# A scan and two MLPs on one core: the due times of the planner's steps moved, and its transfers planned longer

## The chip, the cores and the metric

The kernel runs on one core of a Trainium2 chip. Its engines are TensorE (PE in the profile, with its weight loads as PEld), VectorE (DVE), ScalarE (ACT), GpSimd (POOL) and SyncE (SP), which here issues the transfers. The metric is the device time of one execution in microseconds; three runs of the kernel before have a median of 625.69 us (624.65 to 625.95).

## The reference

```python
def reference(**kwargs):
    attn_out = _attn_ref(x, a, B, C)                     # (4, 8, 768, 32)
    x = attn_out.transpose(0, 2, 1, 3).reshape(3072, 256)
    x = _moe_ref(x, w_in, w_out)       # h = x @ w_in; g = h if h > 0 else exp(h) - 1; g @ w_out   (d_ff 2048)
    return _moe2_ref(x, w_a, w_b, w_out2)                # (x @ w_a * (x @ w_b)) @ w_out2           (d_ff 1536)
```

`_attn_ref` is a linear recurrence over the sequence for 4 batches and 8 heads: state = decay * state + B x, and y = C state, with 16 states and 32 values a head, worked out chunk by chunk: inside a chunk y is (C B^T * L) x with L the decays between two positions under the causal mask, and from the chunk before comes C state times a decay. All is fp32; the second and third part are matrix products over 3072 tokens.

## The kernel before

**The work.** The scan is cut into 24 units u (a chunk of 128 positions, 6 of them, by 4 batches). A unit builds the decays in a tile ab (DVE, L575, two halves), takes their last column (le, ACT, L590) for POOL's product xe (L595), multiplies C and B on PE (L616 for the first 8 units, L629 for the others, four heads at a time, both halves into one PSUM bank, cbank), lets DVE multiply that bank into ab (mask, L632), and forms y and the new state in the bank ybank (L663, L667, L671), from where x is written (L703, or L706 and L709 as a high and a low part). Four units make one tile of 512 tokens of x, and there are 6 tiles. Phase A is the first MLP: each tile has 8 pairs of 256 hidden units; PE's up products (L738, L739, L741: high times high, high times low, low times high; tile 0 in whole fp32, L729), exp on ACT (L837), minus one (L841), the choice of the two branches on DVE (L847), a high part on ACT (L851), a low part on POOL or DVE (L858, L856), and PE's down products into acc (L750, L751, L754). Phase B is the second MLP with Strassen products: 18 groups, each with products of three matmuls (L1139 to L1141) into four banks (ybank, cbank and the two acc), which ACT copies out (keep, L1151) or DVE adds out (plus, L1159); then the gate (L1168, L1171, L1174), the down products (L1079, L1080, L1083), and evictions (L1108, L1110).

**Beside it.** The weights are loaded as raw words into tiles called raw and fx, scaled by ACT (L427, into an m), prepared by ACT or DVE (L434, L430), put together by POOL or DVE (L439), and split into high and low parts (L384, L388). B and C of the units from 8 on are split into bf16 parts as well: a raw load, casts on ACT (L476), rests on POOL (L479), stores into a DRAM tensor called parts (L484, 128 KB each), and from there one load sm a unit (L523, 512 KB). Each unit from 8 on also loads ab from DRAM (L537, 512 KB). PE has filler matmuls for the start (L319).

**What sets the order.** None of this is in the order of the code. The class Plan takes every step (`add`) with a planned length on each engine that could do it, its predecessors and a due time. `emit` then plays the program through with these lengths: of the steps that are ready it picks the one with the smallest `(floor(start / 0.25), due, index)`, gives it to the engine on which it ends first, and writes its instructions at once. So the planned lengths and the due times decide the order of each engine's queue, and each engine executes its queue in that order. What waits at the head of a queue holds up all that is behind it. The table MOVE shifts due times by the part of the program and the step's name; it is empty before. The planned length of a transfer is in the branch for SP: a latency, its KB over 310 and 0.05, one after the other, eight at most outstanding.

Of the kernel before, what the change touches and what calls it, by code (L numbers as in the profile page):

```python
# [63 lines left out]
class Plan:  # L64
# [38 lines left out]
    def emit(self, go=True):  # L103
        n = len(self.steps)
        self.work = {}
        left, then, ends = [0] * n, [[] for _ in range(n)], [None] * n
        for i, s in enumerate(self.steps):
            for a in set(s[2]):
                left[i] += 1
                then[a].append(i)  # L110
        free = dict.fromkeys(("PE", "ACT", "DVE", "POOL", "SP"), 0.7)
        port, dma, done = 0.0, 0.0, 0
        landed = []
        self.log = []
        ready = []

        def enter(i):
            engines, fn, after, due, prt, pad, weight, nb = self.steps[i]
            opts = []
            for e, c in engines.items():  # L120
                at = nb
                for a in after:
                    end, ea = ends[a]
                    end += (self.SYNC[ea] if ea != e else self.SAME[e]) + (pad if ea != e else 0.0)
                    if end > at:
                        at = end
                opts.append((e, c, at))
            ready.append((due, i, opts, prt))

        for i in range(n):  # L130
            if not left[i]:
                enter(i)
        while ready:
            best = None
            for k, (due, i, opts, prt) in enumerate(ready):
                end = None
                for e1, c1, at in opts:
                    s1 = free[e1] if free[e1] > at else at
# [12 lines left out]
            due, _, _, prt = ready.pop(k)  # L151
            if e == "PE":
                if self.fill and go and start < FILL_TO and start - free["PE"] > 0.2:
                    k0 = int(free["PE"] / self.TICK)
                    rate = 1.0 if k0 > 0 and self.work.get(k0 - 1, 0.0) >= 0.5 else 0.5
                    m = int((start - free["PE"] - 0.2) * rate / 0.054)
                    self.fill(m)
                    self.pe_clock(free["PE"], 0.055 * m, 1.0)
                end = self.pe_clock(start, c, self.steps[i][6])
                free[e] = end  # L160
            elif e == "SP":
                end = start
                for kb in c:
                    if len(landed) >= 8:
                        end = max(end, landed[-8])
                    dma = max(dma, end + 1.5) + kb / 310.0 + 0.05
                    landed.append(dma)
                    end += 0.46
                free[e], end = end, dma
            else:  # L170
                end = start + c
                free[e] = end - self.LAG[e]
                if e == "POOL" or prt:
                    port = end
# [14 lines left out]
def kernel(  # L189
# [14 lines left out]
    nc = tc.nc  # L204
# [89 lines left out]
    add = plan.add  # L294
# [166 lines left out]
    def split_bc(m, s, j, due):  # L461
        cols = slice(512 * j, 512 * j + 512)
        rb = raw[1] if s == 1 else nxt(raw, "raw")
        t = rb.ap[:, 0:512].bitcast(F32)
        part = [rb.ap[:, 512 + 256 * i:768 + 256 * i].bitcast(BF16) for i in range(3)]

        slots = ([(0, 3)], [(3, 3)], [(6, 2)]) if m == 0 else ([(0, 3, 2), (6, 0, 0)],) * 3

        def load(e):
            nc.sync.dma_start(t, (bt, ct)[m][P * s:P * (s + 1), cols])  # L470

        last = i_load = add({"SP": [256]}, load, rb.take(), due=due - 8, nb=due - 12)
        rb.users.append(i_load)
        for i in range(3):
            def cast(e, i=i):
                nc.scalar.copy(part[i], t)  # L476

            def rest(e, i=i):
                eng[e].tensor_sub(t, t, part[i])  # L479

            def store(e, i=i):
                dst = parts[s].rearrange("r m (n k) f -> r m n k f", k=8)
                for k in ([[0, 1, 2], [3, 4, 5], [6, 7]][i] if m == 0 else [k for k in range(8) if k % 3 == i]):
                    nc.sync.dma_start(dst[:, m, :, k, cols], part[i])  # L484

            i_c = add({"ACT": 0.62}, cast, last, due=due)
            k = 3 if (i < 2) else 2
            i_s = add({"SP": [128] * k}, store, i_c, due=due)
            i_parts.setdefault(s, []).append(i_s)
            rb.users += [i_c, i_s]  # L490
            if i < 2:
                last = add({"POOL": 1.3}, rest, i_c, due=due, port=True)
                rb.users.append(last)
# [7 lines left out]
    def unit(u, due):  # L501
# [69 lines left out]
        for g in range(2):  # L571
# [71 lines left out]
        if c > 0:  # L643
# [99 lines left out]
    def down(ph, t, f, gh, gl, i_h, i_l, due):  # L743
# [51 lines left out]
    def pair(t, p):  # L795
# [78 lines left out]
        def downs():  # L874
            if quad:
                for f in range(4):
# [6 lines left out]
                    i_down["A", 0] = [add({"PE": 0.89}, dn_q, i3, i_m["w_out", 0], d, due=due + PAIR1 + 0.1 * f)]  # L883
# [513 lines left out]
```

## Time and profile before

| | |
|---|---|
| three runs | 625.69 us median, 624.65 to 625.95 |
| profiled execution | 627.16 us, of which the span of the instructions is 625.5 us |
| PE busy | 608.7 us, 97% of the span |
| ACT, DVE, POOL busy | 375.6, 374.4, 321.6 us |
| mean granted clock of TensorE | 0.991 |
| transfers | 59.94 MB, nearly all in the first 275 us |

The profile is of one execution, so sums over its rows are compared with its own 627.16 us, and its distance to the median (1.47 us) is taken off at the end. PE is busy nearly all of the time, so what is of interest is where it is not, and where its clock is not at 1.00: the page's slices show such places before 200 us and in the last slice. From 275 to 600 us PE has no idle time at all.

### The profile page before, as it was taken

The page shows a single profiled execution, that of the slowest core. Times are in us where ns is not written, and L with a number is a line of the kernel's source. Part 1 is how long each engine was busy: PE and PEld are TensorE (multiplying, and loading weights), DVE is VectorE, ACT ScalarE, POOL GpSimd, SP SyncE. Part 2 cuts the span into 40 slices and gives each one's busy share as a digit, 9 for nine tenths or more (in the row PEclk, how much of TensorE's full clock was granted, in tenths as well). Part 3 has the DMA queues.
Part 4 walks back from the last instruction along what each step waited for, and adds up shares of the span by engine and source line. Part 5 has one row for each costly group of instructions (what it writes and reads, how often), then busy time and mean ns, then how long its engine had stood idle before and what let it go on. Part 6 is the DMA issues. An engine that isn't in the chain of part 4 may idle for free.

```text
span 625.5 us, 9248 instructions
## 1 busy us (share of the span) xinstructions
PE 608.7 (97%) x3533; PEld 480.8 (77%) x3533; DVE 374.4 (60%) x515; ACT 375.6 (60%) x536; POOL 321.6 (51%) x245
## 2 busy tenths in 40 slices
PE   9999997999969999999999999999999999999996
PEld 8864455777857877778888888888888888888885
DVE  7875755876737786788544676556533357433333
ACT  2656575567756757657776765547554456554553
POOL 3353373457755456343452576666555555555552
PEclk9999997999989999999999999999999999999999
DMA  8947743777558655400000000000100000100001
GB/s 250 331 130 256 243 136 118 245 224 242 176 206 301 226 195 193 138 4 1 1 1 0 1 1 1 0 1 1 68 0 2 1 1 1 68 1 0 1 0 68
DMA packets 33404, 59.94 MB, mean 96 GB/s; under 512 B 2736, under 2 KB 13904, under 8 KB 33360
## 3 DMA queue, kind: packets, MB, share of 16 engines
q1 hardware_dynamic: 33360, 59.35, 28.5%
q8 instruction: 28, 0.46, 0.3%
q14 instruction: 16, 0.13, 0.1%
HBM read 47.61 MB, written 11.73 MB: 95 GB/s over the span
## 4 chain that ended last, share of the span: by engine, by line
PE 87%; DMA 5%; ACT 3%; DVE 1%; issue 1%; SPq 1%; POOL 1%; POOLq 0%; ACTq 0%; DVEq 0%
PE acc L754 6%; PE acc L750 6%; PE acc L751 6%; PE up L738 6%; PE up L739 5%; PE up L741 5%; PE up L1083 5%; PE up L1080 5%; PE up L1079 5%; PE acc L1140 4%; PE acc L1141 4%; PE acc L1139 4%; PE ybank L1140 3%; PE cbank L1140 3%; PE ybank L1141 3%; PE ybank L1139 3%
## 5 line engine op out<-in xcount | busy, mean ns | idle before, releaser
L858 POOL TENSOR_TENSOR gl<-e,gh 128x1024 fp32r<-128x1024 f32 x20 | 49.0, 2448 | 62.0 <-ACT gh L851 57.4
L1168 DVE TENSOR_TENSOR x<-x 128x512 f32<-128x512 f32 x36 | 29.0, 807 | 74.2 <-POOL x L1212 73.7
L1174 POOL TENSOR_TENSOR gl<-x,gh 128x512 fp32r<-128x512 f32 x35 | 48.9, 1400 | 35.9 <-ACT gh L1171 35.9
L750 PE MATMUL acc<-gh,hi_w_out 128*128 128x512 f32 x160 | 63.7, 398 | 0.0
L837 ACT ACTIVATE e<-up 128x1024 f32<-128x1024 f32 x44 | 45.1, 1025 | 29.9 <-PE up L741 23.6
L1212 POOL TENSOR_TENSOR x<-e,x 128x512 f32<-128x512 f32 x36 | 45.8, 1292 | 33.4 <-ACT e L1151 29.4
L751 PE MATMUL acc<-gh,lo_w_out 128*128 128x512 f32 x160 | 62.8, 393 | 0.0
L754 PE MATMUL acc<-gl,hi_w_out 128*128 128x512 f32 x160 | 51.8, 400 | 0.0
L841 ACT ACTIVATE e<-e,bias 128x1024 f32<-128x1024 f32 x44 | 50.8, 1154 | 1.0
L575 DVE TENSOR_TENSOR_SCAN ab<-ab,delta 128x512 f32<-128x512 f32 x36 | 49.0, 1372 | 0.4 <-DMA ab<-a_seg 0.4
L847 DVE SCALAR_TENSOR_TENSOR up<-e,up 128x512 f32<-128x512 f32 x40 | 27.8, 695 | 26.5 <-ACT e L841 25.7
L847 DVE SCALAR_TENSOR_TENSOR e<-e,up 128x512 f32<-128x512 f32 x48 | 30.7, 681 | 18.9 <-ACT e L841 18.9
L1174 POOL TENSOR_TENSOR gl<-p,gh 128x512 fp32r<-128x512 f32 x18 | 23.9, 1327 | 34.6 <-issue 31.6
L738 PE MATMUL up<-xh,hi_w_in 128*128 128x512 f32 x96 | 41.2, 430 | 0.0
L739 PE MATMUL up<-xh,lo_w_in 128*128 128x512 f32 x96 | 38.4, 400 | 0.0
L1159 DVE TENSOR_TENSOR p<-acc,p 128x512 f32<-128x512 f32 x36 | 24.3, 688 | 22.0 <-PE acc L1141 22.0
L1079 PE MATMUL up<-gh,hi_w_out 128*128 128x512 f32 x96 | 37.4, 389 | 0.0
L1080 PE MATMUL up<-gh,lo_w_out 128*128 128x512 f32 x96 | 37.4, 389 | 0.0
L632 DVE TENSOR_TENSOR ab<-cbank,ab 128x512 f32<-128x512 f32 x35 | 24.0, 687 | 20.2 <-PE cbank L629 11.9
L750 PEld LDWEIGHTS acc<-gh,hi_w_out 128*128 128x128 f32 x160 | 30.5, 190 | 6.7 <-issue 0.2
L751 PEld LDWEIGHTS acc<-gh,lo_w_out 128*128 128x128 f32 x160 | 30.4, 190 | 6.3
L439 POOL TENSOR_TENSOR m<-m,raw 128x1024 int32<-128x1024 int32 x11 | 27.6, 2511 | 14.1 <-DVE m L430 9.8
(295 smaller groups left out, 1690.5 us busy)
## 6 DMA issues: line engine op xcount, KB each, us to landing
ab<-a_seg SPq DMA_DIRECT2D x18, 512.0 KB
parts<-raw SPq DMA_DIRECT2D x64, 128.0 KB
sm<-parts SPq DMA_DIRECT2D x16, 512.0 KB
p<-in_xb SPq DMA_DIRECT2D x20, 256.0 KB
raw<-in_w_out SPq DMA_DIRECT2D x4, 1024.0 KB
fx<-in_w_out SPq DMA_DIRECT2D x3, 1024.0 KB
out_t<-m SPq DMA_DIRECT2D x12, 256.0 KB
raw<-in_w_in SPq DMA_DIRECT2D x2, 1024.0 KB
```

The source lines that it names most:

```text
L575: nc.vector.tensor_tensor_scan(lt[:, h4].rearrange(flat), lt[:, h4].rearrange(flat) if n else flat4(sp[g]), delta.rearrange(flat), 0.0, op ...
L738: nc.tensor.matmul(ps, w_mm(name, whi, f, c), xh[:, c, :], start=(c == 0), stop=False)
L739: nc.tensor.matmul(ps, w_mm(name, wlo, f, c), xh[:, c, :], start=False, stop=False)
L750: nc.tensor.matmul(accs[m], w_mm(name, whi, f, m), gh, start=(f == 0), stop=False)
L751: nc.tensor.matmul(accs[m], w_mm(name, wlo, f, m), gh, start=False, stop=False)
L754: nc.tensor.matmul(accs[m], w_mm(name, whi, f, m), gl, start=False, stop=(f == last))
L841: nc.scalar.activation(gf, gf, AF.Identity, bias=bias[:, 0:1])
L847: nc.vector.scalar_tensor_tensor(u[:, k, :] if on_dve else gf[:, k, :], gf[:, k, :], 0.0, u[:, k, :], op0=ALU.min, op1=ALU.max)
L1079: nc.tensor.matmul(a4[m].ap, w_mm("w_out2", whi, f, m), gh, start=first, stop=False)
L1080: nc.tensor.matmul(a4[m].ap, w_mm("w_out2", wlo, f, m), gh, start=False, stop=False)
L1140: nc.tensor.matmul(bk.ap, lo_, x[:, 0], start=False, stop=False, **on)
L1174: eng[e].tensor_sub(tap("l" + w), tap(wa), tap("h" + w).bitcast(F32))
```

## The change

Three things change. The empty table MOVE gets some 105 entries, each a shift of the due time of a part's steps by at most 25 us, up or down (the key "" is for all steps of a part, other keys for steps by name; the load of a unit's sm is ld_sm, and so on). The planned transfers become longer. And the planned lengths of some instructions move by a few hundredths of a microsecond. No instruction of the work is added or removed; the fillers go from 41 to 27. All line numbers of the changed kernel are larger by 103 below the table (L629 is L732, L729 is L832).

```diff
 MOVE = {
+    ("bc", (0, 1, 0)): {"": -9.4, "load": 18.2},
...
+    ("unit", 12): {"": -25.0, "st_bd": -20.6},
...
 }
...
-                    dma = max(dma, end + 1.5) + kb / 310.0 + 0.05
+                    dma = max(dma, end + 1.75) + kb / 310.0 + 0.05
...
-            i_s = add({"SP": [128] * k}, store, i_c, due=due)
+            i_s = add({"SP": [250] * k}, store, i_c, due=due)
...
-            i_ab = add({"SP": [512]}, ld_a, ab.take(), i_seg, due=due - ld, nb=due - ld - 10)
+            i_ab = add({"SP": [640]}, ld_a, ab.take(), i_seg, due=due - ld, nb=due - ld - 10)
...
-            i_sm = add({"SP": [512]}, ld_sm, sm.take(), i_parts[s], due=due - ld, nb=due - ld - 10)
+            i_sm = add({"SP": [640]}, ld_sm, sm.take(), i_parts[s], due=due - ld, nb=due - ld - 10)
...
-        i_db = add({"SP": [64]}, ld_db, db.take(), i_run, due=due - ld, nb=due - ld - 10) if c else None
+        i_db = add({"SP": [100]}, ld_db, db.take(), i_run, due=due - ld, nb=due - ld - 10) if c else None
...
-            i_scan.append(add({"DVE": 1.25}, scan, i_ab if n else i_ab[g], i_ones2, due=due, port=n > 0))
+            i_scan.append(add({"DVE": 1.25 if n == 0 else 1.35}, scan, i_ab if n else i_ab[g], i_ones2, due=due, port=n > 0))
...
-                i1.append(add({"PE": 0.89}, dn_w, i_h, i_m[wk], d, i1, due=due))
+                i1.append(add({"PE": 0.865}, dn_w, i_h, i_m[wk], d, i1, due=due))
...
-        i3 = add({"DVE": 1.38}, gg, i2, due=due + 1)
+        i3 = add({"DVE": 1.33}, gg, i2, due=due + 1)
...
-            i5 = add({"DVE": 1.37} if on_dve else {"POOL": 2.45}, lo, i4, gl.take(), due=due + 1,
+            i5 = add({"DVE": 1.3} if on_dve else {"POOL": 2.5}, lo, i4, gl.take(), due=due + 1,
```

The same table in the order of the instructions, at four places.

First, PE at the end of tile 0 of phase A, where the first cbank of unit 8 stands (sm_79 is the tile that the load of the parts fills, up and acc are PSUM banks). Before:

```order
L729 MATMUL acc_120<-f_lo_w_in_98,m_106 128x512
L738 MATMUL up_117<-xh_452,hi_w_in_658 128x512
L739 MATMUL up_117<-xh_452,lo_w_in_786 128x512
L738 MATMUL up_117<-xh_452,hi_w_in_658 128x512
L739 MATMUL up_117<-xh_452,lo_w_in_786 128x512
L741 MATMUL up_117<-xl_456,hi_w_in_658 128x512 x2
L629 LDWEIGHTS sm_79
L629 MATMUL cbank<-sm_79 128x128
```

And now:

```order
L842 MATMUL up_118<-xh_426,lo_w_in_564 128x512
L844 MATMUL up_118<-xl_436,hi_w_in_560 128x512 x2
L841 MATMUL up_118<-xh_426,hi_w_in_560 128x512
L842 MATMUL up_118<-xh_426,lo_w_in_564 128x512
L841 MATMUL up_118<-xh_426,hi_w_in_560 128x512
L842 MATMUL up_118<-xh_426,lo_w_in_564 128x512
L844 MATMUL up_118<-xl_436,hi_w_in_560 128x512 x2
L732 LDWEIGHTS sm_79
L732 MATMUL cbank<-sm_79 128x128
```

Before, the first matmul of cbank came six matmuls after the last one of tile 0 (L729); now it comes 64 matmuls after it (the last L832), of which the rows nearest to cbank are shown.

Second, ACT in the middle of phase A (m2_101 is the scaled weight of w_out, raw0_75 the tile into which its words are loaded, le1_68 the last column of unit 15). Before:

```order
L427 ACTIVATE m2_101<-raw0_75 128x1024
L476 CAST raw1_76<-raw1_76 128x512
L434 ACTIVATE raw0_75<-raw0_75 128x1024
L837 ACTIVATE e0_83<-up0_117 128x1024
L590 COPY le1_68<-ab1_82 128x8
L841 ACTIVATE e0_83<-e0_83,bias_66 128x1024
```

And now, first where le1_68 stands:

```order
L944 ACTIVATE e0_83<-e0_83,bias_66 128x1024
L940 ACTIVATE e1_84<-up1_118 128x1024
L693 COPY le1_68<-ab1_82 128x8
L944 ACTIVATE e1_84<-e1_84,bias_66 128x1024
L579 CAST raw0_75<-raw0_75 128x512
L954 CAST gh0_85<-e0_83 128x1024
```

and then, 14 rows after that le1_68 row, where the scaled weight stands:

```order
L579 CAST raw1_76<-raw1_76 128x512
L944 ACTIVATE e1_84<-e1_84,bias_66 128x1024
L809 CAST xh3_1263<-ybank_115 128x2x128
L530 ACTIVATE m2_101<-raw0_75 128x1024
L954 CAST gh0_85<-up1_118 128x1024
L537 ACTIVATE raw0_75<-raw0_75 128x1024
L940 ACTIVATE e0_83<-up0_117 128x1024
```

Before, the column stood four rows behind the instruction that waits for the load of w_out; now it stands seventeen rows ahead of it.

Third, PE at units 11 and 12 (sm_80 and sm_79 are the two tiles of parts, used in turn; a semaphore named DVE is VectorE's, one named DMAHW a transfer's). Before:

```order
L629 LDWEIGHTS sm_80
L629 MATMUL cbank<-sm_80 128x128
L750 MATMUL acc_119<-gh_85,hi_w_out_740 128x512
L751 MATMUL acc_119<-gh_85,lo_w_out_809 128x512
L750 MATMUL acc_120<-gh_85,hi_w_out_740 128x512
L751 MATMUL acc_120<-gh_85,lo_w_out_809 128x512
L754 MATMUL acc_119<-gl_89,hi_w_out_740 128x512
L754 MATMUL acc_120<-gl_89,hi_w_out_740 128x512
L738 MATMUL up_117<-xh_452,hi_w_in_824 128x512 [waits Activation_49]
```

And now:

```order
L732 MATMUL cbank<-sm_80 128x128
L732 LDWEIGHTS sm_80
L732 MATMUL cbank<-sm_80 128x128
L732 LDWEIGHTS sm_80
L732 MATMUL cbank<-sm_80 128x128
L732 LDWEIGHTS sm_79 [waits DMAHW3_49]
L732 MATMUL cbank<-sm_79 128x128 [waits DVE_49]
L732 LDWEIGHTS sm_79
L732 MATMUL cbank<-sm_79 128x128
```

Before, down and up products followed the second half of unit 11 in cbank; now the first half of unit 12 follows it at once in the same bank, with a wait for DVE and one for a transfer.

Fourth, PE in phase B, where a bank is filled again soon (ybank, cbank and acc are the four banks of the products). Now:

```order
L1242 MATMUL ybank<-op_raw_2190,hs_w_a_2527 128x512
L1243 MATMUL ybank<-op_raw_2190,ls_w_a_2543 128x512
L1244 MATMUL ybank<-op_raw_2190,hs_w_a_2527 128x512
L1242 MATMUL cbank<-op_raw_2262,hi_w_b_2595 128x512
L1243 MATMUL cbank<-op_raw_2262,lo_w_b_2605 128x512
L1244 MATMUL cbank<-op_raw_2262,hi_w_b_2595 128x512
L1242 MATMUL acc_120<-op_raw_2190,hs_w_b_2677 128x512
L1243 MATMUL acc_120<-op_raw_2190,ls_w_b_2682 128x512
L1244 MATMUL acc_120<-op_raw_2190,hs_w_b_2677 128x512
L1242 MATMUL ybank<-op_raw_2262,hi_w_a_2417 128x512
L1243 MATMUL ybank<-op_raw_2262,lo_w_a_2487 128x512
L1244 MATMUL ybank<-op_raw_2262,hi_w_a_2417 128x512
```

The bank ybank is filled, six matmuls go into the two others, and ybank is filled again. Such a refill after six matmuls or fewer stands 34 times among the 248 refills now; before, it stood 3 times.

## Rows read from the trace of the kernel before

**Rows 1.** The page's first lines: busy us of each engine, share, instructions.
```profile
PE 608.7 (97%) x3533; PEld 480.8 (77%) x3533; DVE 374.4 (60%) x515; ACT 375.6 (60%) x536; POOL 321.6 (51%) x245
```

**Rows 2.** Stretches: us, busy of PE PEld DVE ACT POOL (instructions), clock, DMA share, GB/s.
```profile
0.00:25.00 25.00, 23.13 (x268) 20.87 (x269) 20.84 (x30) 11.61 (x22) 10.14 (x18) 1.00 0.89 286
...
100.00:104.00 4.00, 4.00 (x13) 3.23 (x12) 1.89 (x3) 0.83 (x1) 1.95 (x1) 0.50 0.14 53
104.00:108.00 4.00, 4.00 (x18) 2.90 (x18) 1.88 (x3) 1.43 (x3) 0.00 (x0) 0.80 0.12 44
...
180.90:184.90 4.00, 4.00 (x14) 3.29 (x14) 2.33 (x4) 2.99 (x5) 3.96 (x3) 0.60 0.36 117
...
325.00:350.00 25.00, 25.00 (x112) 20.71 (x111) 13.16 (x21) 17.74 (x19) 11.20 (x5) 1.00 0.00 0
275.00:600.00 325.00, 325.00 (x1466) 268.41 (x1465) 173.69 (x237) 192.98 (x299) 174.28 (x122) 1.00 0.02 7
```

**Rows 3.** What PE waited for: us in total, times, longest.
```profile
PE cbank L629 <- DVE ab L632: 4.9, 1, 4.9
PE cbank L629 <- DMA sm<-parts: 3.6, 1, 3.6
PE ybank L663 <- issue: 1.3, 1, 1.3
...
PE ybank L319 <- ACT x L703: 0.8, 1, 0.8
PE up L1083 <- DVE gl L1174: 0.6, 1, 0.6
```

**Rows 4.** PE's timeline at 25 us: start, us, instruction, [idle before <- releaser].
```profile
24.92 1.00 PE L319 MATMUL ybank<-zt 128*128 128x128 bf16 x15 [0.81 <-ACT x L703]
```

**Rows 5.** ACT's timeline before 56 us.
```profile
54.74 1.15 ACT L427 ACTIVATE m<-fx 128x1024 f32<-128x1024 f32 x1 [4.74 <-DMA fx<-in_w_out]
```

**Rows 6.** The chain that ended last, 86 to 100 us: start, us, what.
```profile
90.20 1.19 POOL raw L479
...
91.41 0.63 ACT raw L476
92.05 0.56 SPq L484
...
92.66 3.30 DMA parts<-raw
...
96.18 3.57 DMA sm<-parts
```

**Rows 7.** ACT's timeline, 171 to 181 us.
```profile
176.48 1.12 ACT L427 ACTIVATE m<-raw 128x1024 f32<-128x1024 f32 x1 [4.89 <-DMA raw<-in_w_out]
...
179.01 1.01 ACT L837 ACTIVATE e<-up 128x1024 f32<-128x1024 f32 x1
179.91 0.20 ACT L590 COPY le<-ab 128x8 f32<-128x8 f32 x1
```

**Rows 8.** SP's timeline, 108 to 112 us.
```profile
109.79 0.33 SPq L537 DMA_DIRECT2D ab<-a_seg  x1
```

**Rows 9.** DVE's timeline, 112 to 116 us.
```profile
113.88 2.34 DVE L575 TENSOR_TENSOR_SCAN ab<-ab,delta 128x512 f32<-128x512 f32 x2 [0.39 <-DMA ab<-a_seg]
```

**Rows 10.** DVE's groups by line, 100 to 200 us: busy, mean ns, idle before.
```profile
L632 DVE TENSOR_TENSOR ab<-cbank,ab 128x512 f32<-128x512 f32 x17 | 11.7, 688 | 16.5 <-PE cbank L629 9.9 <-ACT le L590 6.6
L847 DVE SCALAR_TENSOR_TENSOR up<-e,up 128x512 f32<-128x512 f32 x14 | 9.7, 695 | 3.9 <-ACT e L841 3.6
```

**Rows 11.** PE's timeline, 347 to 352 us: a bank filled and filled again.
```profile
348.99 0.39 PE L1141 MATMUL cbank<-op_xl,hi_w_b 128*128 128x512 f32 x1
349.21 0.39 PE L1139 MATMUL ybank<-op_xl,hs_w_a 128*128 128x512 f32 x1
...
350.80 0.39 PE L1139 MATMUL cbank<-op_xl,hs_w_b 128*128 128x512 f32 x1
```

**Rows 12.** ACT's timeline in that stretch.
```profile
349.41 0.59 ACT L1151 COPY p<-cbank 128x512 f32<-128x512 f32 x1 [1.17 <-PE cbank L1141]
350.09 0.59 ACT L1151 COPY x<-ybank 128x512 f32<-128x512 f32 x1
```

**Rows 13.** ACT's groups by line, 325 to 600 us.
```profile
L1171 ACT CAST gh<-x 128x512 fp32r<-128x512 f32 x33 | 20.5, 622 | 12.0 <-DVE x L1168 12.0
```

More of the change, by code (lines that the diff above doesn't have):

```diff
@@ L49 @@
 MOVE = {
+    ("bc", (0, 1, 0)): {"": -9.4, "load": 18.2},
+    ("bc", (0, 2, 0)): {"": -2.7, "load": 5.6},
+    ("bc", (1, 2, 0)): {"": -4.7},
+    ("group", 0): {"": 9.0, "f_t3": -5.6, "ad": 14.8, "hi": -13.5},
+    ("group", 1): {"": -18.7, "mm3": 15.0, "cp": 18.1, "dn_l": 24.7},
+    ("group", 10): {"": -9.7, "mm3": 14.1, "dn_h": 25.0},
+    ("group", 11): {"mm3": 8.9, "dn_h": 17.2},
+    ("group", 12): {"": 9.0, "dn_h": 11.4},
+    ("group", 13): {"mm3": 8.1, "dn_h": 25.0},
+    ("group", 14): {"": 18.4},
@@ new lines @@
+    ("group", 8): {"": -2.8, "dn_l": 10.3, "hi": 8.2},
+    ("group", 9): {"": -11.5, "mm3": 10.8, "dn_h": 25.0},
+    ("late", 2): {"": -16.5, "high": 21.0},
+    ("late", 3): {"": -17.3},
+    ("late", 6): {"high": -1.6},
+    ("late", 7): {"": -12.2, "high": 21.3},
+    ("late", 8): {"": 12.0, "high": 4.6},
+    ("pair", (0, 2)): {"": 25.0},
+    ("pair", (0, 3)): {"dn_q": 25.0},
+    ("pair", (0, 7)): {"up_a": 10.0, "gg": 11.5},
+    ("pair", (1, 0)): {"": 4.8, "hi": -14.2},
+    ("pair", (1, 1)): {"": -18.5},
@@ new lines @@
+    ("pair", (1, 2)): {"": -21.3, "dn_h": 21.5, "up_a": -25.0},
+    ("pair", (1, 3)): {"up_a": -12.4},
+    ("pair", (1, 5)): {"up_a": -21.6},
+    ("pair", (1, 6)): {"dn_h": -25.0, "lo": 25.0},
+    ("pair", (2, 0)): {"": -25.0},
+    ("pair", (2, 1)): {"dn_0": 15.6},
+    ("pair", (2, 2)): {"": 25.0, "dn_l": 20.5},
+    ("pair", (2, 3)): {"lo": -24.7},
+    ("pair", (2, 4)): {"": 13.8},
+    ("pair", (2, 6)): {"dn_l": 21.5},
+    ("pair", (3, 1)): {"up_a": -6.1},
+    ("pair", (3, 4)): {"": 12.1, "dn_h": 21.6},
@@ new lines @@
+    ("pair", (3, 5)): {"up_a": 15.7, "ex": 24.3},
+    ("pair", (3, 6)): {"": 2.2, "up_a": 21.4},
+    ("pair", (3, 7)): {"": -25.0},
+    ("pair", (4, 0)): {"up_a": 0.8, "em": -5.8, "lo": -17.8},
+    ("pair", (4, 1)): {"ex": -19.5},
+    ("pair", (4, 2)): {"dn_h": -22.5},
+    ("pair", (4, 3)): {"": -12.4, "dn_h": -24.0, "lo": 4.3},
+    ("pair", (4, 4)): {"dn_h": -4.9, "up_a": -12.4},
+    ("pair", (4, 5)): {"": 2.3, "up_a": -11.9},
+    ("pair", (4, 6)): {"": -7.9, "up_a": -5.2},
+    ("pair", (4, 7)): {"": -21.2},
@@ new lines @@
+    ("pair", (5, 3)): {"dn_l": 17.9},
+    ("pair", (5, 4)): {"": 16.3, "dn_l": -6.6, "up_a": -12.0},
+    ("pair", (5, 5)): {"dn_h": 16.8, "up_a": 7.3},
+    ("pair", (5, 6)): {"": 15.5, "dn_l": 11.0, "up_a": 8.8},
+    ("split", ("w_in", 0)): {"": -20.7, "high": 5.5, "rest": 22.1},
+    ("split", ("w_in", 1)): {"": 23.4, "high": -16.7},
+    ("split", ("w_in", 2)): {"": -21.9, "high": -0.6},
+    ("split", ("w_in", 3)): {"": -1.4, "high": 11.7},
+    ("split", ("w_out", 0)): {"high": -21.5, "rest": -19.5},
@@ new lines @@
+    ("split", ("w_out", 1)): {"": -3.6, "high": -2.7},
+    ("split", ("w_out", 2)): {"": 13.8},
+    ("split", ("w_out", 3)): {"": 3.1, "high": -1.9},
+    ("unit", 0): {"": 8.4, "x_w": -1.1},
+    ("unit", 10): {"<lambda>": 25.0},
+    ("unit", 11): {"<lambda>": 23.3},
+    ("unit", 12): {"": -25.0, "st_bd": -20.6},
+    ("unit", 13): {"cbm": 24.0},
+    ("unit", 14): {"": 1.3, "ld_sm": 18.9, "ld_x": 23.6, "ld_db": 21.3},
+    ("unit", 15): {"": -16.4, "<lambda>": 19.4},
+    ("unit", 17): {"": -21.4, "ld_sm": 19.2},
@@ new lines @@
+    ("unit", 18): {"ld_db": -5.9, "<lambda>": -6.3},
+    ("unit", 19): {"": -18.4, "<lambda>": 16.9, "st_up": 22.6},
+    ("unit", 2): {"": 5.0, "ld_x": 17.6, "last_col": -16.0},
+    ("unit", 20): {"": -1.3, "ld_sm": 24.2},
+    ("unit", 21): {"": -17.4, "scan": 10.3},
+    ("unit", 23): {"": -9.0, "ld_a": 7.5, "cbm": 18.0},
+    ("unit", 3): {"": 25.0, "ld0": -18.4, "ld_x": -25.0},
+    ("unit", 4): {"": -8.3, "ld0": -2.2, "scan": -10.1, "x_lo": 19.1},
+    ("unit", 5): {"": -1.6, "ld_a": 0.7, "ld0": -2.4, "ld_x": 2.8, "ld_db": 3.0, "xend": -7.3},
@@ new lines @@
+    ("unit", 6): {"": -7.5, "ld_a": 12.3, "ld0": 25.0, "ld_x": 10.0, "ld_db": 18.6},
+    ("unit", 7): {"": -6.5, "ld_a": 19.7, "ld0": -10.9, "ld_x": -14.8, "ld_db": 17.1, "scan": 18.7, "cbm2": 25.0, "<lambda>": 11.6},
+    ("unit", 8): {"": 11.3, "ld_a": 4.0, "ld_sm": -13.7, "ld_x": 9.3, "ld_db": 18.0, "cbm": 19.7},
+    ("unit", 9): {"ld_a": 9.0, "ld_x": 19.2, "scan": 15.7, "cbm": 14.1},
+    ("w", ("w_in", 0)): {"": -12.1},
+    ("w", ("w_in", 1)): {"load": -18.2, "put": -5.6},
+    ("w", ("w_in", 2)): {"last3": -20.7},
@@ new lines @@
+    ("w", ("w_in", 3)): {"": 19.2, "load": -3.6, "shift": -13.0},
+    ("w", ("w_out", 0)): {"": -7.7, "last3": 2.7},
+    ("w", ("w_out", 1)): {"": -6.1, "load": 6.3},
+    ("w", ("w_out", 2)): {"": -3.9, "load": 2.4, "put": 25.0},
+    ("w", ("w_out", 3)): {"": -9.1, "load": 4.7},
+    ("wb", ("w_a", 0)): {"put": -24.9},
+    ("wb", ("w_a", 2)): {"": -1.5, "load": 6.7},
+    ("wb", ("w_b", 2)): {"shift": 25.0},
+    ("wb", ("w_out2", 0)): {"last3": 22.8},
+    ("wb", ("w_out2", 1)): {"": 24.2},
@@ L50 @@
+    ("wb", ("w_out2", 2)): {"": 12.3, "load": -12.8},
+    ("xset", 1): {"": 21.7, "f_t3": -25.0, "x_l": 12.2},
+    None: {"": -23.6},
 }
@@ L652, in unit @@
             i_sbd = add({"POOL": 0.82}, st_bd, i_state[b], sbd.take(), i_heads, due=due, port=True)
-            i_cd = add({"POOL": 0.72}, lambda e: nc.gpsimd.tensor_mul(cd, cd, dbt), i_p, i_db, due=due, port=True)
+            i_cd = add({"POOL": 0.7}, lambda e: nc.gpsimd.tensor_mul(cd, cd, dbt), i_p, i_db, due=due, port=True)
             sbd.users.append(i_sbd)
@@ L882, in downs @@
                     d = accb[0].take() + accb[1].take() if (p, f) == (0, 0) else i_down["A", 0]
-                    i_down["A", 0] = [add({"PE": 0.89}, dn_q, i3, i_m["w_out", 0], d, due=due + PAIR1 + 0.1 * f)]
+                    i_down["A", 0] = [add({"PE": 0.865}, dn_q, i3, i_m["w_out", 0], d, due=due + PAIR1 + 0.1 * f)]
                     eb_.users += i_down["A", 0]
```

9 lines of the change are left out of this document (added).

## The prediction, made before the changed kernel ran

> **What bounds the kernel now.** I read the page's busy times first: PE is busy 608.7 us [rows 1] of a span of 625.5 us, and no other engine is above 376 us. So PE is the bound, and the time is what PE must do plus what it stands still plus what it loses at the low clock. The stretches say where that can be [rows 2]: from 275 to 600 us PE is busy 325.00 of 325 us, and the clock there is 1.00. Nothing can be won there with the same matmuls. What can be won lies before about 200 us and in the tail. Third, the waits of PE [rows 3]: five places, of 4.9, 3.6, 1.3, 0.8 and 0.6 us (a sixth, before the first matmul, is the start itself). Fourth, for each of them the timeline of the engine waited for, to see what stood at the head of its queue:
>
> a) At 24.9 us PE waits 0.81 us for ACT and then runs 15 fillers, 1.00 us [rows 4]. Those stand where no work was ready.
> b) The 1.35 us before L663 come from ACT, whose L427 stood 4.74 us at the head of the queue for the load of w_out [rows 5]; the last columns and x parts of the unit were behind it.
> c) The 3.56 us at 96.2 us are a chain: rest on POOL, cast, the store's issue, 3.30 us until the store landed, 3.57 us until sm landed, and then cbank [rows 6]. PE had nothing else that could go. The next 4 us ran at clock 0.50 and the 4 after at 0.80 [rows 2].
> d) The 4.94 us before 180.9 us name DVE's mask, but the mask waited for the column le, and that stood on ACT behind an L427 that waited 4.89 us for w_out, then a cast, a preparation and an exp, so that le ran at 179.91 [rows 7]. The 4 us after it ran at 0.60 [rows 2].
> e) The 0.64 us in the tail: PE's L1083 waits for DVE's L1174, which stands in DVE's queue behind an eviction.
>
> **The change part by part.** The work is the same, so each term is one of these losses, or a new one. All are against the profiled execution, 627.16 us.
>
> a) DVE is busy 20.84 of the first 25 us and moves no work away, so the start is only partly PE's. Between nothing and 0.81 + 1.00 = 1.81 us can go; 14 fillers fewer speak for a part of it. I take the middle: 0.9.
>
> b) 1.35, gone if ACT's L427 is not in front of the unit's work before its words are there. In SP's queue that load of w_out stood behind the eight stores of a quarter (L484); now it stands ahead of all eight, and on ACT two more pairs' exps stand in front of the L427. I take 1.35; the lower bound is 0, if another L427 is late in its place.
>
> c) The chain from cast to landing is not shorter, so the wait goes only if PE has work to do meanwhile. The order shows that it has: between the last L729 matmul of tile 0 and the first cbank of unit 8 there were 6 matmuls, and there are 64 now. Eight matmuls start in 350.80 - 348.99 = 1.81 us, 0.226 each [rows 11], so 58 more are 13 us of work. The last cast is later as well, by about 3.5 to 5 us of PE's work, so a margin of some 13 - 5 - 3.6 = 4 us is left. The gain is the wait and the half clock after it: 3.56 + 4 x (1 - 0.50) + 4 x (1 - 0.80) = 3.56 + 2.0 + 0.8 = 6.36. The lower bound is 0, if the store and load take 4 us more than here.
>
> d) The column le of unit 15 stands seventeen rows ahead of the L427 on ACT instead of four behind it, and the load of w_out is issued some 10 us of planned work ahead of its need. A late w_out would now hold up ACT's casts and exps, not the mask. The gain is 4.94 + 4 x (1 - 0.60) = 4.94 + 1.6 = 6.54; the lower bound is 0.
>
> e) 0.64: in the new order no eviction stands in front of that L1174.
>
> The gains are 0.9 + 1.35 + 6.36 + 6.54 + 0.64 = 15.79.
>
> f) What it adds. At units 11 and 12 the first half of unit 12 follows the second half of unit 11 in cbank at once. The mask of unit 11 must read the bank in between: 0.69 us, and DVE has a pair of L847 ahead of that mask, 2 x 0.695 [rows 10]. So PE waits from 0.69 + 0.1 = 0.8 us to 0.69 + 1.39 + 0.1 = 2.2 us; behind the waiting cbank stand unit 12's state products and then all of phase A's matmuls. I take 2.0, near the upper end, since DVE is in order and that pair stands there. Whether the clock falls: after a wait of 1.35 us it did not, after 3.56 us it did [rows 2, 3]. The first is nearer, so no; a fall would add up to 2.8 as in c.
>
> g) The transfers. An ab load was issued at 109.79 and its scan began at 113.88 [rows 8, 9], 4.1 us. A unit has to wait for it if its ab buffer comes free less than that before its scan is due. From PE's order the least distance between the two units that share a buffer is 9.3 us of matmuls (9.8 before, with no wait), so ab has room. The sm load takes 3.57 us, and its least distance is 5.4 us now (9.7 before): room of 1.8 us. Some transfer will still be late where two or three are issued together. I take half of the smallest wait seen, 0.7; between 0 and 3.6, the largest.
>
> h) Phase B refills a bank after six matmuls or fewer 34 times, where it was 3 times. In one of the three, the last matmul into cbank starts at 348.99 and takes 0.39, the copy on ACT runs 349.41 to 350.00, and the next matmul into the bank starts at 350.80 [rows 11, 12]: PE is not held. The refill comes 8 x 0.226 = 1.81 us after that start, and what lies between is 0.39 + 0.04 + 0.59 + 0.04 + some 0.2, so about 0.5 us are to spare. If ACT is in the middle of another instruction of 0.62 us [rows 13], half of it on average, 0.3, still fits; two in front do not. The cost is 0, from 0 to 34 x 0.68 = 23, of which the rivals speak. ACT is busy 192.98 of 325 us there [rows 2].
>
> That stretch runs at clock 1.00 with PE moving from bank to bank [rows 2, 11]. The Trainium skill, "TensorE: Matmul & The Clock Gate", section "A second HAM failure mode: psum-queue depth-cycling", says that a kernel which cycles through PSUM banks can leave PE idle between groups of matmuls for so short a time that the matmuls look the same while the clock falls and comes back; it speaks against 34 tighter refills. By the row the term is 0; by the rule it would be the half clock again, up to 2.8 us for each place where PE is held, and no row of this case has such a place in phase B.
>
> The planned lengths alone cost nothing; only the order that follows from them does. They now lie nearer to the trace: two stores and their landing took 92.05 to 95.96, 3.9 us, and sm 3.57 [rows 6], where a store of 128 KB was planned with 1.5 + 128/310 + 0.05 = 1.96 and now 2.6, and sm with 3.2 and now 3.9.
>
> The costs are 2.0 + 0.7 = 2.7, so the net is 15.79 - 2.7 = 13.1: 627.16 - 13.1 = 614.1 for an execution like the profiled one. That one is 1.47 above the median of the three, so the median comes to **612.6 us**.
>
> **The rivals.**
> First, a transfer wait moves instead of going: one of c and d comes back at another unit, with its half clock. For it: the order was found with planned lengths, and the chain of c is as long as before while 16 sm loads and 64 stores share a queue. Against it: the margins of 4 us and of 17 rows. Time: 612.6 + 6.4 = 619.0.
> Second, the other side: phase B's refills wait. Two ACT instructions in front of the copy, 0.62 + 0.59 us, exceed the spare 0.5 by 0.68 us; in all 34 places that is 23 us, and the kernel would be at 612.6 + 23.1 = 635.7. It decides from 13.1 / 34 = 0.39 us a refill. For it: ACT is the engine with the most work there and the splits of weights (about 1 us each) are in its queue too. Against it: the three refills of before cost nothing, and only every seventh refill of the 248 is a tight one.
> Third, the change does not do what it says: the waits come from something other than the order (a transfer that is simply late), and the time stays at 625.7. For it: every wait named a transfer in the end. Against it: w_out was late at the head of ACT's queue while PE's work stood behind, and that is order.
>
> **How the numbers follow.** Forecast, all big waits gone: 0.74. One of the two back: 0.18. Refills wait: 0.05. Nothing: 0.03. A run of this kernel can tell about 0.2%, 1.25 us. The first two are faster and the refill rival slower: faster 0.92, and 0.01 more from refills that lose less than 0.39 each; slower is the rest of that rival, 0.04, and 0.01 of the last case; the same is 0.02 of the last case. The range: the best is all of a and no costs, 627.16 - 16.70 - 1.47 = 609.0. Upward it takes in the rival of one wait back, with 1 us for a fallen clock at f: 620.0.
>
> **What the profile of the changed kernel would show.** Right: PE's waits before 200 us shrink from 11 us to about 3, the largest at units 11 and 12 in cbank with DVE as releaser and about 2 us; no stretch of 4 us at clock 0.50; L427's successor on ACT without a wait of 4 us in front of a column; PE busy near 603 us, since the matmuls at half clock are gone; phase B still without idle time. Wrong: a wait of PE for sm<-parts or ab<-a_seg of 3 us or more; slices of phase B in which PE is below its full share or the clock below 1.00, with waits for ACT's L1151; or a start that is longer than before, with PE waiting for DVE.

## The result and the profile after

The changed kernel takes 615.54 us (median of 4 runs, 614.65 to 618.82) against 625.33 for the kernel before (4 runs, 624.65 to 625.95): a ratio of 0.9857, 95% interval 0.9823 to 0.9892. Forecast were 612.6, between 609.0 and 620.0. A fifth execution of after took 617.37 us. The profiled one took 618.82 us, with a span of 615.9: 2.9 us of it lie outside the span of the instructions, where every other execution of this study has 1.7 to 1.9 us there.

The busy times of the page answer to [rows 1]:

```profile
PE 608.0 (99%) x3519; PEld 481.0 (78%) x3519; DVE 374.2 (61%) x516; ACT 373.6 (61%) x533; POOL 322.0 (52%) x247
```

PE's idle time is 615.9 - 608.0 = 7.9 us, where it was 16.8. What PE waited for, to be read beside [rows 3]:

```profile
PE cbank L732 <- DVE ab L735: 1.5, 1, 1.5
PE ybank L422 <- POOL zt L418: 1.1, 1, 1.1
```

Of the five waits of before none is left, and one is new. The second line is the wait before the first matmul. The stretches of after (columns as in [rows 2]):

```profile
0.00:25.00 25.00, 23.59 (x229) 21.07 (x230) 16.80 (x27) 7.43 (x16) 6.10 (x16) 0.80 0.88 250
...
9.00:12.00 3.00, 2.87 (x31) 2.45 (x29) 1.18 (x2) 1.52 (x4) 1.59 (x1) 0.81 0.93 247
12.00:15.00 3.00, 3.00 (x15) 3.00 (x15) 2.88 (x5) 0.00 (x0) 1.36 (x2) 0.50 0.85 222
15.00:18.00 3.00, 3.00 (x26) 2.52 (x28) 1.95 (x2) 0.00 (x0) 0.00 (x0) 0.50 0.94 296
18.00:21.00 3.00, 3.00 (x32) 2.64 (x30) 1.26 (x2) 1.62 (x4) 1.19 (x2) 0.50 1.05 363
21.00:24.00 3.00, 3.00 (x53) 2.57 (x54) 2.27 (x3) 1.52 (x3) 0.62 (x1) 0.98 1.02 271
...
100.00:104.00 4.00, 4.00 (x19) 3.29 (x19) 1.54 (x3) 3.77 (x6) 1.17 (x1) 1.00 0.46 144
...
175.00:200.00 25.00, 25.00 (x188) 20.07 (x187) 18.28 (x25) 18.14 (x23) 15.98 (x15) 1.00 0.73 239
...
275.00:600.00 325.00, 325.00 (x1465) 268.19 (x1466) 168.38 (x234) 193.13 (x305) 179.24 (x127) 1.00 0.02 7
```

Where c and d were, the clock is 1.00 and PE has no gap, and phase B is as full as before. But in the first 25 us the clock is 0.80 where it was 1.00: PE is busy there, at 1.2 GHz. That costs 3 x (0.19 + 3 x 0.50 + 0.02) = 5.1 us in this execution. Two signs of the forecast failed with it: there is a stretch at clock 0.50, of 9 us, and PE is busy 608.0 us where about 603 was expected. Without the 5.1 it would be 602.9.

The one wait, on the timelines of PE (first two rows) and then of DVE:

```profile
136.30 0.38 PE L732 MATMUL cbank<-sm 128*128 128x128 bf16 x4
138.22 0.38 PE L732 MATMUL cbank<-sm 128*128 128x128 bf16 x4 [1.54 <-DVE ab L735]
```

```profile
136.16 1.42 DVE L950 SCALAR_TENSOR_TENSOR up<-e,up 128x512 f32<-128x512 f32 x2
137.48 0.68 DVE L735 TENSOR_TENSOR ab<-cbank,ab 128x512 f32<-128x512 f32 x1
```

These are units 11 and 12. The mask could have read the bank from 136.68 on, but the pair of L950 stood ahead of it in DVE's queue. It is the place, the cause and nearly the size of step f.

One more view bears on the explanation below: the waits of every engine, between 30 and 275 us, that name a transfer (engine, what <- transfer: us in total, times, longest us). The largest of them before:

```profile
POOL p L653 <- DMA p<-in_xb: 11.6, 4, 3.5
ACT raw L476 <- DMA raw<-in_ct: 5.5, 2, 4.0
ACT m L427 <- DMA raw<-in_w_out: 5.4, 2, 4.9
POOL xe L595 <- DMA db<-a_dec: 5.3, 2, 4.4
ACT m L427 <- DMA fx<-in_w_out: 4.7, 1, 4.7
```

and after:

```profile
POOL p L756 <- DMA db<-a_dec: 5.6, 3, 2.6
ACT raw L579 <- DMA raw<-in_ct: 2.8, 2, 1.7
ACT m L530 <- DMA raw<-in_w_out: 2.6, 2, 1.6
DVE ab L678 <- DMA ab<-a_seg: 2.2, 1, 2.2
```

All rows of this kind add up to 53.4 us before (13 rows) and 19.0 after (10 rows). Of the 53.4, 23.2 are ACT's, 21.4 POOL's, 0.4 DVE's; only 3.6 are PE's own and 4.8 its weight loads'.

### The profile page after: what moved, and what is told of

Read it like the earlier page. It is cut to its first block, busy times and chain, and to the rows that moved or that the text cites. A ratio compares the mean times of both kernels' runs of the same rounds, so it can differ in the third digit from the quotient of the medians.

```text
span 615.9 us, 9231 instructions
## 1 busy us (share of the span) xinstructions
PE 608.0 (99%) x3519; PEld 481.0 (78%) x3519; DVE 374.2 (61%) x516; ACT 373.6 (61%) x533; POOL 322.0 (52%) x247
## 4 chain that ended last, share of the span: by engine, by line
PE 97%; DMA 1%; DVE 1%; SPq 0%; issue 0%; POOL 0%; ACT 0%; POOLq 0%
PE up L841 6%; PE acc L857 6%; PE acc L853 6%; PE up L842 6%; PE up L844 6%; PE acc L854 6%; PE up L1182 5%; PE up L1186 5%; PE up L1183 5%; PE acc L832 5%; PE up L832 5%; PE acc L1242 4%; PE acc L1244 4%; PE acc L1243 4%; PE ybank L1244 3%; PE cbank L1244 3%
## 5 line engine op out<-in xcount | busy, mean ns | idle before, releaser
L1277 POOL TENSOR_TENSOR gl<-x,gh 128x512 fp32r<-128x512 f32 x35 | 47.2, 1354 | 53.6 <-ACT gh L1274 52.2
L961 POOL TENSOR_TENSOR gl<-e,gh 128x1024 fp32r<-128x1024 f32 x20 | 50.5, 2523 | 43.5 <-ACT gh L954 33.5
L1271 DVE TENSOR_TENSOR x<-x 128x512 f32<-128x512 f32 x36 | 30.9, 866 | 33.6 <-POOL x L1315 33.2
L1274 ACT CAST gh<-x 128x512 fp32r<-128x512 f32 x36 | 22.4, 622 | 33.9 <-DVE x L1271 25.8
L950 DVE SCALAR_TENSOR_TENSOR up<-e,up 128x512 f32<-128x512 f32 x40 | 27.7, 693 | 22.6 <-ACT e L944 21.8
L1262 DVE TENSOR_TENSOR x<-acc,x 128x512 f32<-128x512 f32 x36 | 24.4, 685 | 27.3 <-PE acc L1244 27.3
L950 DVE SCALAR_TENSOR_TENSOR e<-e,up 128x512 f32<-128x512 f32 x48 | 30.6, 678 | 13.6 <-ACT e L944 13.5
```

The costliest lines, as they stand in the source:

```text
L950: nc.vector.scalar_tensor_tensor(u[:, k, :] if on_dve else gf[:, k, :], gf[:, k, :], 0.0, u[:, k, :], op0=ALU.min, op1=ALU.max)
L1277: eng[e].tensor_sub(tap("l" + w), tap(wa), tap("h" + w).bitcast(F32))
```

## The experiments

Each run is compared with runs of the kernel before on the same chip. Their medians were 625.6, 626.5, 625.9 and 626.7 us in the four groups, each with single executions some 5 to 8 us apart.

**The parts of the change.** First the new planned lengths without any moved due time:

```diff
 MOVE = {
-    ("bc", (0, 1, 0)): {"": -9.4, "load": 18.2},
...
 }
```

> The new planned lengths with an empty table of due times. In the order that comes out, 88 matmuls stand between the end of tile 0 and the first cbank of unit 8 (6 before, 64 after), and the column of unit 15 stands nine rows ahead of the scaled weight of w_out on ACT; the start has the small loads ahead of the weight, as before, with 39 fillers. Theory 1 (what counts is which work stands in front of c's and d's transfers, and the lengths alone put it there): both large waits go, 625.3 - 6.4 - 6.5 = 612.4, with up to 3 us of smaller waits that come or stay, 612 to 616; no low clock in the first 25 us. Theory 2 (the moved due times bring the gain, the lengths are only their base): 622 to 626, with a wait of 3 us or more at a cbank.

Measured: 621.13 us, ratio 0.9932 (0.9913 to 0.9952). Between the theories: the two large waits are gone, 53 us of waits for transfers became 18.9, but PE now waits for other engines:

```profile
PE cbank L629 <- DVE ab L632: 2.2, 3, 1.3
PE up L738 <- ACT xh L706: 2.2, 1, 2.2
...
PE ybank L319 <- ACT x L703: 1.1, 1, 1.1
PE acc L754 <- POOL gl L858: 1.0, 2, 0.7
PE up L738 <- DVE gl L856: 0.9, 1, 0.9
PE cbank L1139 <- ACT p L1151: 0.5, 1, 0.5
```

The opposite half, the table with the old lengths (its diff is the table alone):

> The table of due times with the old planned lengths. 24 matmuls stand before unit 8's first cbank, the column of unit 15 one row ahead of the scaled weight, the weight's load ahead of the small loads at the start as after, 40 fillers, 34 tight refills in phase B. Theory 1: 18 matmuls more are 4.1 us of work against a wait of 3.56 that moves later with the last cast, so c goes by half or comes back whole, d goes: 625.3 - 6.5 - 0 to 6.4 + 0 to 4 for the start's clock = 613 to 622. Theory 2: 612 to 616, near the changed kernel.

Measured: 645.08 us, ratio 1.0312 (1.0260 to 1.0364), slower than before and outside both expectations. The waits for transfers are 71.1 us, and PE waits for the other engines:

```profile
PE acc L857 <- POOL gl L961: 5.3, 3, 4.2
PE up L841 <- DVE m L950: 4.0, 1, 4.0
PE ybank L766 <- DVE f_hi_w_out L735: 3.8, 1, 3.8
```

So the due times by themselves cost 19.5 us. That they fit only the order that comes out of the new lengths is a reading of this, not shown entry by entry.

Of the table, phase A's entries alone (those for group, wb, xset and late left out), with the new lengths:

> The changed kernel without the due times of the second MLP's groups, weights and late splits: the order of phase A is that of after (64 matmuls, unit 15's column thirteen rows ahead), and phase B has 5 tight refills instead of 34. Theory 1 (refills cost nothing): within 1 us of the changed kernel, 614.5 to 617, with the low clock at the start. Rival (34 refills cost something): faster by the part of 29 x 0.39 us that they lose, 605 to 614, which phase B's slices of the changed kernel without idle time speak against.

Measured: 623.51 us, ratio 0.9966 (0.9930 to 1.0001), some 8 us slower than the whole change, which neither theory had. From 25 to 250 us PE stands still nearly as little as in after; the loss lies later. In 250 to 275 us PE is busy 23.17 of 25 us, at clock 0.93, and it loses time behind that too, where the kernel before and the whole change are full:

```profile
275.00:600.00 325.00, 321.73 (x1457) 264.51 (x1449) 170.40 (x229) 187.28 (x297) 182.60 (x129) 0.99 0.02 7
```

Of the 3.27 us there, 3.1 are two waits at acc, for POOL's gl (2.1) and ACT's gh (1.0). With 5 tight refills in place of 34 phase B is not faster, so the refills are not what the whole change loses by.

And phase B's entries alone, with the new lengths:

> The changed kernel with the due times of the second MLP alone: phase A's order is that of the lengths alone (88 matmuls), 30 tight refills in phase B, the start as before. Theory 1: the time of the run with lengths alone within 1 us, 612 to 616. Theory 2: 622 to 626.

Measured: 620.21 us, ratio 0.9931 (0.9903 to 0.9960), within 1 us of the lengths alone, as theory 1 had it, although 30 tight refills stand in it: its 300 to 600 us are busy for 299.81.

Last, the five lengths of transfers alone, with the old lengths of instructions:

```diff
-                    dma = max(dma, end + 1.5) + kb / 310.0 + 0.05
+                    dma = max(dma, end + 1.75) + kb / 310.0 + 0.05
...
-            i_s = add({"SP": [128] * k}, store, i_c, due=due)
+            i_s = add({"SP": [250] * k}, store, i_c, due=due)
```

> The kernel before with the five planned lengths of transfers alone (latency 1.75, stores 250, sm and ab 640, db 100); the lengths of instructions are the old ones and the table is empty. 84 matmuls stand before unit 8's first cbank (88 with all lengths). Theory (the transfers' lengths bring the transfers in time, the due times then remove the short waits of one engine for another): the engines' waits that name a transfer between 30 and 275 us fall to about 20 us as with all lengths (53 before), no wait of PE for sm, and the time is that of all lengths alone, 619 to 623. Rival (the lengths of the instructions matter as much): 624 to 626, with a wait of 3 us or more that names a transfer at the head of ACT's queue.

Measured: 619.67 us, ratio 0.9893 (0.9856 to 0.9931); the waits for transfers are 16.9 us, none of them PE's for sm. The lengths of the transfers are what brings the transfers in time; those of the instructions add nothing to it here.

Together: against the kernel before on the same chip, the transfers' lengths alone gain 7.0 us, all lengths alone 4.5 and the whole change 9.8. The first two differ by no more than their intervals allow. What the table adds on top of the lengths came only with the whole of it: phase A's half lost 2.4 us against the lengths alone, and phase B's half gained 0.9. Which of its entries work together stays open.

**c and d one at a time, in the kernel before.** A list holds single steps back in the order of emission until a later step has been emitted, with all that depends on them; the plan itself stays.

```diff
+HOLD = [({272}, 379), ({274}, 380), ({278, 304}, 376), ({306}, 378), ({310, 350}, 412)]
...
-                self.steps[i][1](e)
+                self.put(i, e)
```

> The kernel before, with the cbank matmuls of units 8 to 10 emitted 8 to 24 PE matmuls later (30 matmuls stand between the end of tile 0 and unit 8's first cbank instead of 6; transfers and all else in the old order). Theory 1 (c is lack of cover): the 3.56 us wait for sm and the half clock after it go, since 24 matmuls are 5.4 us of work: 625.6 - 6.4 = 619.2; the 4.9 us of d stay. Rival (the late transfer holds up something else first, so the wait moves to another line): 623 to 626, with a wait of 2 us or more within 20 us of it.

Measured: 626.73 us, ratio 1.0004 (0.9983 to 1.0025). This run doesn't answer: the load of unit 10's decays was emitted ahead of unit 8's last use of the same tile, so unit 8's y is made from unit 10's decays, and it waits for that load. The same with that load kept behind:

> The kernel before, with the cbank matmuls of units 8 to 10 emitted 8 to 24 PE matmuls later, and what follows from them kept behind them; transfers in the old order. Theory 1 (c is lack of cover at one place): the 3.56 us wait and its half clock go, 626 - 6.4 = 619.6 against a kernel before at 626. Rival, after the run on d, in which 4.2 of 6.5 us came back 12 and 20 us later (the transfers themselves are issued too late, and the next user waits): most of the wait shows up again as waits of 1 us or more at cbank or acc between 100 and 125 us, and the time is within 2 us of before.

Measured: 623.47 us, ratio 0.9962 (0.9937 to 0.9986), a gain of 2.4 where the wait and its half clock would be 6.4. The cbank of unit 8 no longer waits for sm, but on PE's timeline, 10 us behind it:

```profile
113.18 0.42 PE L684 MATMUL ybank<-ab,p 128*32 128x128 f32 x8 [1.21 <-DVE ab L649]
...
116.74 0.38 PE L646 MATMUL cbank<-sm 128*128 128x128 bf16 x4 [0.33 <-DVE ab L649]
```

The mask of the first row stands behind a scan on DVE, which waits for the next ab:

```profile
DVE ab L592 <- DMA ab<-a_seg: 2.2, 1, 2.2
```

From 90 to 125 us PE idles 2.1 us in all instead of 3.6, and the clock is 1.00. So the half clock is gone, and more than half of the wait is back.

With d, the steps held are the scaling, its neighbours on ACT and what follows from them (`HOLD = [({619, 581, 621}, 632)]`):

> The kernel before, with the scaling of w_out2's first quarter, the cast and the preparation behind it emitted after the pair's next three ACT instructions (exp, minus one, high part), so that the column of unit 15 no longer stands behind the load; PE's and SP's orders are those of before. Theory 1 (d is the order of ACT's queue): the 4.9 us wait goes with its half clock: 625.6 - 6.5 = 619.1; c's 3.56 stay. Rival (the load is late whatever stands behind it, and the next cast or high part waits instead): 623 to 626.

Measured: 626.05 us, ratio 1.0003 (0.9978 to 1.0028): no gain. The column ran at 173.66 and the wait of 4.9 us is gone, but on PE's timeline behind it:

```profile
187.11 0.73 PE L771 MATMUL acc<-gl,hi_w_out 128*128 128x512 f32 x2 [1.56 <-POOL gl L875]
189.46 0.47 PE L755 MATMUL up<-xh,hi_w_in 128*128 128x512 f32 x1 [0.24 <-DVE gl L873]
195.78 0.40 PE L646 MATMUL cbank<-sm 128*128 128x128 bf16 x4 [2.44 <-DMA sm<-parts]
```

1.56 + 0.24 + 2.44 = 4.24 us of the 6.5 are back within 20 us. The cast behind the scaling is the head of the chain of stores to the next sm: that load was issued at 189.40 us, where it was 189.66 before, so it came no later than before, but PE came earlier. The rest, 2.3, lies inside what single executions differ by. The run on d speaks for the rival: a late transfer, taken out of one engine's way, holds up its next user. The run on c lies between the theories, with the next user (the scan) held up and the clock kept.

**The start.** In the changed kernel the first two sets of C and B products (16-row matmuls, L719) stand side by side at 8.4 to 11.9 us, and the clock fell there. 24 fillers more, 12 ahead of each set:

```diff
                 if n:
                     plan.fill = None
+                elif u < 2:
+                    warm(12)
```

> The changed kernel with 12 more fillers ahead of each of the first two sets of C and B products (the two sets stood side by side at 8.4 to 11.9 us, and the clock was 0.50 from there to 21 us in the profiled execution). Theory (the sparse start lets the clock fall in some executions): clock 1.00 from 9 to 25 us, the 5.1 us lost there go against at most 24 x 0.055 = 1.3 us of fillers: 613.7 to 615.0 in every run, less spread than 614.65 to 618.82. Rival (those 16-row matmuls lower the clock by themselves): 616 to 620, the clock still 0.50 there.

Measured: 614.58 us (5 runs, 614.35 to 614.80), ratio 0.9819 (0.9798 to 0.9841). The start runs at full clock:

```profile
9.00:12.00 3.00, 2.96 (x44) 2.56 (x43) 1.82 (x3) 2.39 (x4) 0.39 (x1) 1.00 0.54 167
12.00:15.00 3.00, 3.00 (x33) 2.70 (x32) 2.09 (x4) 0.00 (x0) 2.57 (x2) 1.00 0.78 191
15.00:18.00 3.00, 2.89 (x47) 2.48 (x48) 2.67 (x4) 0.64 (x3) 0.45 (x1) 1.00 0.99 375
18.00:21.00 3.00, 3.00 (x52) 2.67 (x50) 3.00 (x4) 2.65 (x5) 1.36 (x3) 1.00 1.02 380
```

The mean clock was 0.991 to 0.997 in five executions of the changed kernel; in the five with fillers it was 0.998 to 1.000. The other runs agree: in the first 25 us the clock was 1.00 with the lengths alone and with phase B's due times, whose start is as before, and 0.93 and 0.86 with phase A's due times and with the due times alone, which have the weight's load in front of the small ones as after does. This is the shortest time of the study, but its interval overlaps that of the changed kernel. Two more tried to take the wait of f as well, by emitting the mask ahead of the pair of L950 (`HOLD = [({474}, 397)]`):

> The same, and on DVE the mask of unit 11's second half emitted ahead of the pair of L950 instead of behind it. Theory (f is that pair): the one wait of PE, 1.54 us for the mask, becomes 1.54 - 0.76 = 0.8 us, and the time is 0.7 us below that of the run with fillers alone. Rival (the pair's delay of 0.7 us holds up the down products instead): the same time, with a new wait of 0.7 us on a high part.

Measured: 615.65 us (615.53 to 615.84), 1.07 slower than with fillers alone. The wait shrank as expected, and the other theory's price came too:

```profile
PE up L860 <- ACT xh L828: 1.6, 1, 1.6
...
PE cbank L751 <- DVE ab L754: 0.8, 1, 0.8
```

The pair, 1.0 us later than with fillers alone (134.53 against 133.49), put off ACT's high part, and with it the scaling behind it and unit 11's x_hi. So that scaling was held behind x_hi too (`HOLD = [({474}, 397), ({516, 518}, 402)]`):

> The changed kernel with the 24 fillers, the mask of unit 11 ahead of the pair of L950 on DVE, and the scaling and preparation of w_b's first quarter behind unit 11's x_hi on ACT, behind which x_hi stood late in the run before. Theory: the 1.58 us wait of PE for x_hi goes and the wait for the mask stays at 0.8: 615.65 - 1.58 = 614.1, 0.5 below the run with fillers alone. Rival (the next wait takes its place, as in the run before): 614.6 to 615.6.

Measured, on another chip: 615.36 us (615.01 to 615.38): PE still waits 1.2 us for x_hi, the rival. And the same, on that chip, with 6 fillers instead of 12 in each place:

> The same with 6 fillers in each place instead of 12. Theory (half of the fillers hold the clock too): 0.66 us fewer fillers, of which PE's idle time at the start takes a part: 613.4 to 614.1 in every run. Rival (6 are too few, the clock falls in some executions): runs up to 618.

Measured: 615.35 us (614.38 to 616.08). The clock was 0.996 to 1.000, so 6 hold it nearly as well, but nothing is gained by them.

## Why the prediction came out as it did

The time lies in the range, 2.9 us above the forecast, and the likeliest case, all large waits gone, is the one that came. By its steps, of the profiled executions:

| step | forecast | after |
|---|---|---|
| a, start | 0.9 gained | 3.7 lost: 0.5 less idle, 14 fillers of 0.067 less [rows 4], 5.1 at half clock |
| b, L663 | 1.35 gained | gone |
| c, sm of unit 8 | 6.36 gained | gone, clock 1.00 |
| d, column of unit 15 | 6.54 gained | gone, clock 1.00 |
| e, tail | 0.64 gained | gone; the stretch from 600 us on idles 0.45 more besides |
| f, units 11 and 12 | 2.0 lost | 1.54 lost |
| g, other transfers | 0.7 lost | none on PE |
| h, tight refills | 0 | 0: 325.00 of 325 us busy, clock 1.00 |

The measured column adds up to -3.7 + 1.35 + 6.36 + 6.54 + 0.64 - 0.45 - 1.54 = 9.2. Its rows lie within the spans, and these differ by 625.5 - 615.9 = 9.6; 0.4 us stay unexplained. The two times differ by 8.34 only, because of what the profiled execution of after has outside its span.

The step that was wrong is **a**, and by its sign: I bounded it from below by nothing, because I asked only what PE waited for at the start. The new order puts the first weight load (1 MB) in front of the small loads. The first products of C and B ran at 8.44 us, where it was 6.75 before, and the sm of the second set landed at 10.03, so the two sets of 16-row products stand side by side. From the chain that ended last (first row) and PE's timeline of after:

```profile
3.63 6.40 DMA sm<-in_bc
...
6.07 2.27 PE L654 MATMUL acc<-a,delta 128*128 128x128 f32 x16
8.44 1.51 PE L719 MATMUL up<-sm 16*128 16x128 f32 x16
...
11.93 3.78 PE L654 MATMUL acc<-a,delta 128*128 128x128 f32 x16
```

Sixteen matmuls of L654 take 2.27 us ahead of the two sets and 3.78 behind them. PE's idle time hardly changed; its clock did. The premise on DVE was wrong as well: it moved work away, with 16.80 us busy in the first 25 where it had 20.84. The loss is not in every execution: of five of after, two had a mean clock of 0.991 (spans 615.7 and 615.9) and three of 0.996 or 0.997 (612.9 to 614.4). Put a, with the result known, in the middle between 5.1 lost and 0.9 gained, and the forecast becomes 612.6 + 3.0 = 615.6; that it then meets the median is chosen, not forecast.

**c** was right in its mechanism and its size. From SP's timeline and PE's:

```profile
106.82 0.90 SPq L626 DMA_DIRECT2D sm<-parts  x2
...
113.88 0.40 PE L732 MATMUL cbank<-sm 128*128 128x128 bf16 x4
```

The first cbank runs without a wait, 7.1 us after the loads are issued. If sm landed in 3.57 us as before [rows 6], the margin is 3.5, where 4 was forecast; the landing itself is not seen, since nothing waited for it.

**d** went, but the reason given was half of it. I read the wait as one of ACT's order. The run on d alone shows that the order isn't enough: 4.2 us came back behind it. That d went as forecast is in part luck. In the changed kernel the load stands elsewhere as well. Before, it was issued at 170.46 and landed 6.0 us later (176.48, [rows 7]), with a run of eight stores of parts behind it (from 178.13); now it is issued at 182.18, with such a run in front of it (from 174.51), and ACT's scaling finds it nearly there. From the timelines of SP and ACT:

```profile
182.18 0.39 SPq L523 DMA_DIRECT2D raw<-in_w_out  x1
...
189.14 1.13 ACT L530 ACTIVATE m<-raw 128x1024 f32<-128x1024 f32 x1 [1.00 <-DMA raw<-in_w_out]
```

So the 10 us of room that I had counted between the load's issue and its use were 7.0, and 1.0 of waiting was left. (The weight is a part of the second MLP's w_out2, whose name the trace cuts short, not of the first's w_out, as the text ahead of the prediction has it.)

**f** was right in place, cause and size. That it could be taken out cheaply was not: each move of it brought a wait of 1.2 to 1.6 us elsewhere.

**h** was right: with 34 refills after six matmuls or fewer PE had no gap from 275 to 600 us, and the clock was 1.00. That holds for this order. In the run with the due times alone, with the same number of tight refills, PE waited 1.6 us in all at ybank and cbank for ACT's copies (L1254). The Trainium skill, "TensorE: Matmul & The Clock Gate", section "A second HAM failure mode: psum-queue depth-cycling", puts the loss of clock down to short idle times of PE between groups of matmuls. In the changed kernel's phase B the trace shows no such idle time, so what the section warns of did not arise.

Of the rivals, the first (a transfer wait moves instead of going) is what happens in the kernel before when d is mended alone, and in part when c is; it did not happen in the changed kernel, where the transfers as a whole are earlier than their users: 53.4 us of waits for them became 19.0. The lengths of transfers do that alone (16.9, and 626.7 - 619.67 = 7.0 us of gain by the medians of that group); the due times then take away PE's short waits for other engines, 7.9 in the run with all lengths (its rows without the wait before the first matmul), 1.5 in the whole. The third rival (nothing happens) and the second (refills) did not come.

## What to carry to other kernels

When an order is worked out from planned lengths, put in the lengths that the trace shows for transfers, landing and all, before anything else is searched: here five numbers gave 7.0 us, where the whole change gave 9.8, and 103 entries of due times without them made the kernel 3% slower. A wait for a late transfer is not worth its length until its next user has been looked at: of two such waits, worth 6.4 and 6.5 us with the half clock behind them, removed singly, 2.4 and nothing were gained. Where a new order touches the start, read the clock there and not only the idle time, and look at more than one execution.

## What the runs showed of the hardware

PE was busy 2.87 to 3.00 of every 3 us from 9 to 21 us in after, and its clock was 0.81 and then 0.50; before, with the same kinds of matmul in another order, it was 1.00. Idle time alone does not account for that: PE idled 0.36 us from 3 to 12 us in after, while 1.35 us of idle time between 56 and 60 us in before left the clock at 1.00. The clock also differed between executions of the same program. The spread of a kernel's times is no measure of its waits for transfers: 22 runs of the kernel before (53.4 us of such waits) lay between 622.26 and 629.16, and the five with fillers (9.8 us) within 0.45 us, but ten with phase A's due times (20.1 us) lay 6.9 us apart.
